# A state-space layer and its MLP on one Trainium2 core: B and C in buffers kept for the whole kernel, the identity written into them once, and a new table of priorities

## The chip, the cores and the metric

The kernel runs on one core of a Trainium2 chip. The figure of merit is device time in microseconds for one execution, the median of several. Engines are named as the profile names them: PE is TensorE's matmuls, PEld its weight loads, DVE is VectorE, ACT is ScalarE, POOL is GpSimd, SP is SyncE, whose queue (SPq) issues every transfer here.

## The reference

A chunked state-space recurrence for 4 batches x 8 heads x 768 positions, head width 32, state width 16, followed by an MLP on the 3072 x 256 result. Cut to what matters:

```python
cum = np.cumsum(log(a) in the chunk)
L = np.exp(cum[:, None] - cum[None, :]) * causal
M = (C @ B.T) * L                       # within a chunk
y = M @ x + (C @ state) * exp(cum)      # plus what the state brings in
state = exp(sum) * state + sum_j B_j x_j * exp(cum_last - cum_j)
h = y_all @ w_in                        # 256 -> 2048
out = (h - np.tanh(h)) @ w_out          # 2048 -> 256
```

## The kernel before

**Tiling.** A batch's 768 positions are cut into 7 chunks of 112 (the last has 96), 28 chunks in all. A chunk uses all 128 partitions: 112 are its positions, and the first 16 rows are the 16 state dimensions. So one matmul with 128 rows of weights gives both the part within the chunk and what the state brings in. To make that work, the tile of B, which is 128 columns wide, starts with a 16 x 16 identity, and columns 16 to 127 hold B transposed.

**Groups.** Two chunks form a group (CPG = 2, 14 groups). For each group four kinds of input are loaded: `bc` (B and C transposed, four transfers of 16 partitions each, line 301), `x` (313), `braw` (B with positions on partitions, 322). Three buffers each go round (NGB = 3). In `prep`, POOL writes the identity into the group's freshly landed `bc` (line 410) and multiplies `braw` by the decay into `bw` (403).

**One chunk.** PE forms the differences of the summed logarithms and C times B into `att` (lines 516 and 525; 454 and 466 for the first three chunks), ACT takes the exponential (540; 473), DVE multiplies (544; 478), POOL applies the causal mask (547; 483), and PE forms the outputs and the next state in `y` (573, 579). ACT copies the state into rows 0 to 15 of the next chunk's `x` (584) and rounds the outputs into `xh` (597); DVE forms the remainder `xl` (602). This is a recurrence: a chunk's `y` needs the copies of the one before.

**The MLP.** Weights arrive as 64-bit numbers, 512 KB a transfer in two transfers for each of 8 steps (`raw`, line 332), and ACT and DVE take them apart into high and low parts (`conv`: ACT 355 and 376, DVE 360, 365, 368, 372, 379). For a tile of 256 positions and a step, PE forms `ph` with 12 matmuls (650), ACT and DVE form g, its high part and its remainder (665, 669, 673, 680), and PE adds 12 matmuls into `o` (725). The first tile's first two steps work in plain float32 (634, 706) from `whole` (590). The first four tiles sweep over the steps in pairs while the later weights are still being converted; the other eight tiles run all steps at once.

**Order.** Every operation is first recorded with a cost in `Order`; `schedule` runs a list schedule over the recorded costs and lags with a priority for each operation, taken from its position plus the number in the table `RANK`; instructions are then written out in the order of the planned starts. Where the plan leaves a lull on PE in its first 65 us, `fill` writes small matmuls of ones without use (441) into the program. All waits between engines are put in by what each instruction reads and writes.

**The start.** ACT needs the clipped decays `a_sb` (DVE line 829) for the logarithm `la` (865); PE sums them (892, 897) behind a run of warming matmuls (859); DVE cuts the sums into three parts (904 to 908) which go out to memory and come back as `lt_c` and `rt_c` (911, 917, 919). POOL sets `lt_c` to ones first (852) and copies the identity `idn` into the three `braw` (847).

Of the kernel before, what the change touches and what calls it, by code (L numbers as in the profile page):

```python
# [9 lines left out]
F32 = mybir.dt.float32  # L10
# [9 lines left out]
P = 128  # L20
# [11 lines left out]
CPG = 2  # L32
# [19 lines left out]
57 373 306 52 13 1164 287 241 205 13 1206 343 161 1190 1241 114 367 108 1133 277 1199 243 1269 127 4 207 264 311 328  # L52
321 1175 105 167 330 1110 262 116 217 1141 -38 182 221 104 385 262 549 591 1114 142 276 81 79 1077 98 -9 99 1225 1080
508 155 398 226 39 277 1079 972 54 25 713 -51 1136 437 15 103 540 476 45 212 1093 244 173 438 53 580 176 -12 1038 -73
149 88 1035 -60 69 -5 -54 855 -93 560 1115 107 -10 956 -50 122 -89 142 247 41 -29 959 93 1159 800 26 -102 1047 -97 -3
1136 1104 1025 1118 217 1141 1062 -118 90 51 -67 456 1051 125 1050 923 1126 -69 240 437 133 1088 703 755 978 -16 1135
1112 -113 355 1087 1137 969 46 228 -115 967 1086 213 -4 6 172 158 991 151 983 181 1002 5 999 14 995 -120 37 -15 376
329 -91 -20 991 1026 1018 1081 1052 5 987 -80 339 -87 1021 1011 -184 -123 -164 123 -9 933 -1 -118 1078 -128 991 -82
-154 286 176 -45 -109 -147 843 915 -128 -102 -182 -161 944 119 713 1014 -115 1016 968 -179 5 90 811 -203 -2 141 -163
-135 1030 1013 64 -146 93 100 265 298 -195 1051 7 -169 -7 -168 114 977 -26 -63 -227 87 -57 -138 -119 1022 13 -69 -212  # L60
55 -244 473 -125 868 -158 -252 -209 253 451 523 961 -191 919 982 -20 -228 554 -148 -5 -196 -72 -274 -271 56 -257 76
-45 941 355 -251 839 848 841 -253 61 770 16 -241 -188 -5 726 -29 95 -237 668 -153 -269 989 893 836 908 -96 981 -248
-167 972 -208 -177 936 -85 -308 908 -317 48 916 -64 -60 -72 -136 -130 15 940 -50 -110 916 -221 -33 -309 61 952 -179
-77 857 280 869 24 -49 921 -277 242 -256 -18 -239 -255 941 -135 923 801 -332 816 -41 563 788 -181 -191 -304 -363 -89
-16 -268 817 -245 873 870 898 913 -26 835 -251 -300 -261 -134 884 898 433 240 867 -368 755 93 -163 883 439 -58 -111
179 763 -173 -194 -348 -391 791 -101 824 56 -376 -343 -285 -299 806 842 218 -353 577 -242 790 -298 -39 -350 226 -118
-40 -174 -34 -179 27 131 479 -160 840 -187 -283 114 806 -220 -234 384 96 -341 729 -407 779 -279 44 -20 -276 189 -369
-305 583 -280 -191 -403 768 795 768 -421 833 -70 736 -418 825 -75 -245 -296 386 -346 696 -352 792 666 -4 745 -220 683
-284 772 -463 -307 -104 232 -123 -49 -245 -226 650 -132 -387 -304 -284 704 -279 -289 -82 -298 -163 -176 249 700 -119
-325 -426 -240 -391 -227 -192 52 -294 -330 -205 -164 651 713 -148 34 226 -286 -3 -432 267 -250 676 -377 757 -366 612  # L70
-240 -251 713 -277 648 648 733 628 -442 510 -484 739 278 744 694 -502 -298 643 688 -116 569 74 -224 -269 -478 511 718
698 -469 101 112 -336 252 475 -324 400 572 613 485 694 -377 -244 553 50 -208 -339 -341 287 -335 -291 236 246 -151 -167
57 137 570 206 -109 -148 -259 324 509 -242 -454 194 -248 -253 -299 -445 -245 -431 -313 615 -116 -102 -471 -316 576
-334 -373 549 512 -367 -285 -262 488 -195 -449 308 -142 156 -301 506 -171 -258 359 -18 264 283 -501 -159 -147 -338
-355 33 189 -198 -163 -267 -240 -315 -198 230 215 150 216 -335 -277 -269 -248 -237 -264 -193 -286 -238 -260 -258 549
12 -479 150 508 518 -216 535 147 39 -279 -274 283 288 282 290 -296 -278 -272 -271 -270 -281 -286 -270 -270 -265 -265
-280 -277 -267 -264 -264 -264 -281 -279 -264 -264 -261 -258 -483 -448 -607 -365 -367 -409 442 -556 -494 196 22 -423
530 436 497 -420 -511 434 -401 471 -294 -291 -279 -278 -276 -273 -291 -288 -275 -274 -270 -269 -286 -283 -273 -271
-270 -267 -284 -281 -269 -268 -259 -258 -591 -212 -460 -599 -547 -436 -560 -437 68 405 -289 -278 -277 268 273 267 274
-289 -278 -276 -274 -270 -286 -291 -276 -273 -271 -270 -315 -157 -350 -55 -396 -134 -309 -89 -46 -332 -243 412 -227  # L80
375 359 -279 475 399 -109 154 490 499 -684 121 -310 -304 -296 -295 -293 -292 -305 -303 -293 -291 -290 -288 -305 -304
-288 -288 -286 -283 -297 -270 -269 -271 -270 -287 -284 -296 -291 -281 -309 -305 -291 -290 -279 -278 -306 -303 -280
-277 -272 -268 -298 -294 -280 -276 -271 -269 -292 -255 -253 -252 -252 -258 -256 -271 -268 -264 -160 -142 -142 -139
-152 -142 -150 -138 -118 -112 355 391 -133 -111 -312 -299 -298 214 221 213 224 -313 -301 -301 -299 -297 -307 -313 -297
-295 -286 -283 -309 -306 -287 -286 -285 -283 -305 -301 -285 -285 -284 -281 -299 -263 -261 -261 -259 -283 -281 -283
-279 -272 -304 -302 -295 -294 -291 -289 -303 -302 -287 -284 -277 -272 -301 -296 -274 -272 -268 -267 -295 -290 -275
-272 -268 -267 -290 -247 -247 -245 -247 -252 -250 -268 -262 -259 -168 -159 -168 -159 -167 -160 -167 -160 -114 -107
-638 -410 -151 -107 -306 -296 -298 131 141 133 143 -308 -298 -298 -296 -295 -305 -310 -291 -290 -281 -278 -306 -301
-280 -279 -279 -278 -300 -297 -280 -280 -279 -277 -293 -272 -268 -265 -261 -256 -295 -293 -285 -283 -277 -271 -294
-292 -269 -269 -264 -263 -288 -280 -265 -265 -262 -261 -280 -274 -265 -260 -246 -245 -277 -256 -254 -254 -253 -258  # L90
-256 -274 -270 -266 -153 -142 -151 -143 -150 -141 -150 -144 -99 -91 -624 -202 -140 -90 -295 -283 -282 54 63 54 65 -295
-277 -277 -275 -273 -290 -296 -274 -272 -268 -265 -289 -252 -252 -252 -252 -257 -253 -275 -269 -263 -295 -292 -274
-269 -260 -259 -289 -284 -261 -257 -255 -252 -281 -276 -254 -252 -246 -242 -273 -235 -235 -235 -234 -257 -255 -252
-248 -245 -279 -273 -253 -250 -243 -242 -269 -261 -243 -242 -236 -235 -261 -258 -245 -243 -236 -230 -256 -212 -212
-211 -208 -217 -215 -230 -228 -223 -262 -251 -251 -25 -15 -21 -13 -265 -253 -249 -246 -242 -255 -266 -243 -240 -231
-229 -255 -251 -231 -229 -227 -225 -252 -248 -227 -226 -225 -223 -243 -203 -203 -202 -204 -223 -223 -222 -219 -213
-250 -244 -237 -236 -230 -227 -244 -243 -227 -225 -218 -215 -242 -236 -217 -214 -209 -208 -236 -232 -218 -216 -210
# [9 lines left out]
class Order:  # L107
# [70 lines left out]
    def lag(self, a, b):  # L178
        if a == "DMA":
            return {"POOL": 2.4, "DVE": 1.3, "ACT": 1.3}.get(b, self.DMA_LATENCY)  # L180
# [851 lines left out]
```

## Time and profile before

| | us |
|---|---|
| median of 3 runs (332.73 to 334.93) | 333.41 |
| the profiled execution's own time | 334.76 |
| span of its profile | 333.1 |
| PE busy in the span | 325.3 (98%) |
| DVE, ACT, POOL busy | 226.6, 191.1, 57.8 |

The span runs from the first to the last instruction; the execution's own time has 1.66 us beside it. Ends of matmuls are modelled, so a busy PE also holds useless matmuls and short pauses. The granted clock of PE is 1.00 (2.4 GHz) in every slice.

### The profile page before, as it was taken

To read this page: it belongs to the slowest core of one execution; us is meant where nothing else is said; L and a number is where in the kernel's file an instruction comes from. 1 tells how busy PE (TensorE), PEld (TensorE's weight loads), DVE (VectorE), ACT (ScalarE), POOL (GpSimd) and SP (SyncE) were. 2 spreads that over 40 slices of the span, in tenths; PEclk is the share of its full clock that TensorE was granted. 3 is DMA by queue.
4 is the path that set the end of the run, shared out by engine and by line. 5 is a ranking of instruction groups with operands and counts; after the bars stand their busy time and mean duration, and the time that the engine had idled before them with its cause. 6 is when DMAs were issued, how large, how long until landed. Compare 5 with 4: busy or idle time off the path is not lost.

```text
span 333.1 us, 9055 instructions
## 1 busy us (share of the span) xinstructions
PE 325.3 (98%) x3864; PEld 312.4 (94%) x3864; DVE 226.6 (68%) x330; ACT 191.1 (57%) x404; POOL 57.8 (17%) x74
## 2 busy tenths in 40 slices
PE   8988999999999999999999999999999999999995
PEld 6976789899999999999999999999999999999995
DVE  5699999998899966555555755655655655654542
ACT  4876888885655655444535744644655645643441
POOL 8355446320002110100001201101111101100000
PEclk9999999999999999999999999999999999999999
DMA  6959579731001202200001200200100100000000
GB/s 176 237 158 281 126 197 268 202 124 40 3 9 37 64 0 75 70 31 2 31 2 32 65 22 10 65 9 24 63 2 3 34 2 2 31 2 2 31 2 32
DMA packets 12472, 21.41 MB, mean 64 GB/s; under 512 B 2848, under 2 KB 7648, under 8 KB 12432
## 3 DMA queue, kind: packets, MB, share of 16 engines
q1 hardware_dynamic: 12432, 20.84, 22.1%
q8 instruction: 30, 0.49, 0.7%
q14 instruction: 10, 0.08, 0.1%
HBM read 17.51 MB, written 3.32 MB: 63 GB/s over the span
## 4 chain that ended last, share of the span: by engine, by line
PE 82%; DMA 7%; DVE 3%; SPq 3%; ACT 2%; issue 1%; ACTq 0%; DVEq 0%
PE ph L650 36%; PE o L725 34%; DMA raw<-w_d 4%; DMA bc<-bc_d 3%; PE y L573 3%; PE att L525 2%; PE o L718 2%; PE att L718 2%; PE cp L454 1%; PE att L516 1%; SPq L332 1%; SPq L301 1%; SPq L917 1%; PE y L579 1%; DMA a_sb<-a_d 1%
## 5 line engine op out<-in xcount | busy, mean ns | idle before, releaser
L669 DVE TENSOR_TENSOR g<-ph,g 128x512 f32<-128x512 f32 x96 | 65.9, 690 | 54.0 <-ACT g L665 53.8
L665 ACT ACTIVATE g<-ph 128x512 f32<-128x512 f32 x96 | 57.5, 599 | 74.0 <-PE ph L650 72.7
L650 PE MATMUL ph<-xh,wh 128*128 128x256 f32 x376 | 95.5, 279 | 0.4 <-DVE g L669 0.3
L650 PE MATMUL ph<-xh,wl 128*128 128x256 f32 x376 | 94.6, 276 | 0.0
L680 DVE TENSOR_TENSOR gl<-g,gh 128x512 fp32r<-128x512 f32 x94 | 65.5, 699 | 26.3 <-ACT gh L673 24.5
L673 ACT CAST gh<-g 128x512 fp32r<-128x512 f32 x94 | 58.1, 620 | 33.6 <-DVE g L669 30.8
L650 PE MATMUL ph<-xl,wh 128*128 128x256 f32 x376 | 73.2, 276 | 0.0
L650 PEld LDWEIGHTS ph<-xh,wh 128*128 128x128 f32 x376 | 70.6, 188 | 1.1 <-DVE g L669 0.7
L650 PEld LDWEIGHTS ph<-xh,wl 128*128 128x128 f32 x376 | 70.6, 188 | 0.0
L547 POOL TENSOR_SCALAR_AFFINE_SELECT lt<-lt 128x896 f32<-128x896 f32 (+1 forms) x25 | 27.2, 1087 | 173.0 <-DVE lt L544 160.2
L650 PEld LDWEIGHTS ph<-xl,wh 128*128 128x128 f32 x376 | 56.6, 188 | 0.0
L725 PE MATMUL o<-gh,wh 128*128 128x256 f32 x344 | 55.0, 282 | 0.0
L725 PE MATMUL o<-gh,wl 128*128 128x256 f32 x344 | 53.0, 276 | 0.0
L725 PE MATMUL o<-gl,wh 128*128 128x256 f32 x344 | 53.0, 276 | 0.0
L725 PEld LDWEIGHTS o<-gh,wh 128*128 128x128 f32 x344 | 45.5, 188 | 0.9
L725 PEld LDWEIGHTS o<-gh,wl 128*128 128x128 f32 x344 | 45.4, 188 | 0.0
L725 PEld LDWEIGHTS o<-gl,wh 128*128 128x128 f32 x344 | 45.4, 188 | 0.0
L544 DVE TENSOR_TENSOR lt<-att,lt 128x896 f32<-128x896 f32 (+1 forms) x25 | 26.6, 1065 | 2.6 <-ACT lt L540 2.1
L540 ACT ACTIVATE lt<-att 128x896 f32<-128x896 f32 (+1 forms) x25 | 22.6, 903 | 2.3 <-PE att L525 1.5
L584 ACT COPY x<-y 16x64 f32<-16x64 f32 x96 | 19.5, 203 | 6.2 <-DVE xl L602 3.2
L403 POOL TENSOR_TENSOR bw<-braw,wdec 128x256 f32<-128x256 f32 x14 | 12.7, 913 | 48.4 <-PE y L579 43.1
L573 PE MATMUL y<-lt,x 128*32 128x112 f32 (+1 forms) x448 | 16.3, 263 | 1.1 <-POOL lt L547 0.7
(93 smaller groups left out, 305.1 us busy)
## 6 DMA issues: line engine op xcount, KB each, us to landing
raw<-w_d SPq DMA_DIRECT2D x16, 512.0 KB
x<-x_d SPq DMA_DIRECT2D x14, 256.0 KB
bc<-bc_d SPq DMA_DIRECT2D x56, 60.0 KB
out_d<-ob SPq DMA_DIRECT2D x16, 128.0 KB
braw<-bn_d SPq DMA_DIRECT2D x14, 112.0 KB
out_d<-pt SPq DMA_DIRECT2D x8, 128.0 KB
cum<-parts SPq DMA_DIRECT2D x1, 168.0 KB
lt_c<-cum SPq DMA_DIRECT2D x4, 27.0 KB
```

The lines of the kernel that those rows point to most:

```text
L540: nc.scalar.activation(k["l"][:, :, 0:q].rearrange("p (i w) q -> p i w q", i=4), place[1][:, :, 0:2, N : N + q], AF.Exp)
L544: nc.vector.tensor_tensor(out=lt, in0=place[1][:, :, 2:4, N : N + q], in1=lt, op=ALU.mult)
L547: nc.gpsimd.affine_select(out=k["l"][:, :, 0:q], in_=k["l"][:, :, 0:q], pattern=[[0, H], [1, q]], compare_op=ALU.is_ge, fill=0.0, base=N, ...
L573: nc.tensor.matmul(out=y[D * h : D * h + D, hg * Q : hg * Q + q], lhsT=d["x"][:, cg, P * hg + D * h : P * hg + D * h + D], rhs=k["l"][:, 4 ...
L584: nc.scalar.copy(grp[(ck + 1) // CPG]["x"][0:N, (ck + 1) % CPG, 2 * D * i : 2 * D * i + 2 * D], k["y"][D * i : D * i + N, H * D : H * D + ...
L650: nc.tensor.matmul(out=ph[:, j, :], lhsT=w_[:, u, 0, k, j * P : (j + 1) * P], rhs=d[("xh", "xl")[p]][:, k, ts], start=p == 0 and k == 0 an ...
L665: nc.scalar.activation(g, gs[t, u][0], AF.Tanh)
L669: nc.vector.tensor_tensor(out=g, in0=ph, in1=g, op=ALU.subtract)
L673: nc.scalar.copy(gh, gs[t, u][1])
L680: on.tensor_tensor(out=gl, in0=g, in1=gh.bitcast(F32), op=ALU.subtract)
L718: nc.tensor.matmul(out=halves[e], lhsT=(wh, wl, wh)[k][:, u, 1, j, e * P : (e + 1) * P], rhs=(gh, gh, gl)[k][:, j, :], start=u == seg[0] a ...
L725: nc.tensor.matmul(out=po[t, seg][:, e, :], lhsT=w_[:, u, 1, j, e * P : (e + 1) * P], rhs=g[:, j, :], start=u == seg[0] and k == 0 and j = ...
```

## The change

The three `bc` buffers become tiles of the constant pool that stay for the whole kernel, laid out as two halves x two chunks x (128 + 112) columns: B's 128 columns with the identity in the first 16, and C's 112 behind. POOL writes the identity once into all three, near the start (`beside`). The fourteen copies in `prep` go. A transfer now brings 4 runs of 224 numbers (896 bytes) for each partition instead of one of 960 (3840 bytes). The recorded lag from a transfer to an operation other than POOL, DVE and ACT becomes 1.2 instead of 0.8, and the table `RANK` has other numbers and fewer of them.

```diff
 RANK = """
-57 373 306 52 13 1164 287 241 205 13 1206 343 161 1190 1241 114 367 108 1133 277 1199 243 1269 127 4 207 264 311 328
...
+124 176 146 114 265 79 304 288 100 21 511 230 42 126 213 329 -6 99 792 241 121 151 359 114 161 243 136 137 209 171
...
         if a == "DMA":
-            return {"POOL": 2.4, "DVE": 1.3, "ACT": 1.3}.get(b, self.DMA_LATENCY)
+            return {"POOL": 2.4, "DVE": 1.3, "ACT": 1.3}.get(b, 1.2)
...
-        d["n_bc"] = slot("bc", NGB)
+        d["n_bc"], d["bc"] = slot("bc", NGB), bcs[G % NGB]
 
         def fn(i):
-            if i == 0:
-                d["bc"] = p2.tile([P, 2, CPG * (P + Q)], F32, tag="bc", name=f"bc{G}", bufs=NGB)
-            nc.sync.dma_start(out=d["bc"][32 * i : 32 * i + N], in_=bc[G, i])
+            nc.sync.dma_start(out=d["bc"][32 * i : 32 * i + N, :, :, N:], in_=bc[G, i])
...
-        def fn_c():
-
-            bb = d["bc"][:, :, 0 : CPG * P].rearrange("p w (c m) -> p w c m", c=CPG)
-            nc.gpsimd.tensor_copy(out=bb[:, :, :, 0:N], in_=idn.unsqueeze(1).unsqueeze(1).broadcast_to([P, 2, CPG, N]))
-
-        op("POOL", 0.38, fn_c, r=["idn"], w=[d["n_bc"]])
...
-        bb = d["bc"][:, :, c * P : (c + 1) * P]
-        cc = d["bc"][:, :, CPG * P + c * Q : CPG * P + (c + 1) * Q]
-        return bb, cc
+        return d["bc"][:, :, c, 0:P], d["bc"][:, :, c, P:]
...
-        return [grp[ck // CPG]["n_bc"], l_c[s], r_c[s]]
+        return [grp[ck // CPG]["n_bc"], "ci", l_c[s], r_c[s]]
...
+    bcs = [cp.tile([P, 2, CPG, P + Q], F32, name=f"bc{i}") for i in range(NGB)]
...
+    def beside():
+
+        for t in bcs:
+            nc.gpsimd.tensor_copy(out=t[:, :, :, 0:N], in_=idn.unsqueeze(1).unsqueeze(1).broadcast_to([P, 2, CPG, N]))
+
+    op("POOL", 1.5, beside, r=["idn"], w=["ci"])
```

**Where instructions move.** The orders of the two programs differ little over most of their length; the chunks 11 to 15 come later on PE, behind more of the MLP's matmul groups. The three places below are in the first part of the program. Numbers behind a name tell one tile from another.

First place, SP at the program's start. Before:

```order
L817 DMA a_sb<-a_d 112x192
L301 DMA bc_130<-bc_d 16x960
L819 DMA a_sb<-a_d 96x32
L313 DMA x_133<-x_d 128x512
L313 DMA x_143<-x_d 128x512
L301 DMA bc_130<-bc_d 16x960 x3
L322 DMA braw_99<-bn_d 112x256
L332 DMA raw_150<-w_d 128x1024 x2
L301 DMA bc_159<-bc_d 16x960 x4
```

Now:

```order
L294 DMA bc_102<-bc_d 16x4x224
L802 DMA a_sb<-a_d 112x192
L804 DMA a_sb<-a_d 96x32
L315 DMA braw_99<-bn_d 112x256
L325 DMA raw_132<-w_d 128x1024 x2
L294 DMA bc_102<-bc_d 16x4x224 x3
L306 DMA x_144<-x_d 128x512
L306 DMA x_146<-x_d 128x512
L294 DMA bc_103<-bc_d 16x4x224 x4
```

The two transfers of the first weights (`raw`) stand ahead of three of the four pieces of the first `bc` and of the first two `x`; before, they stood behind them all.

At the same place POOL, before:

```order
L821 IOTA pid 128x2
L822 IOTA ncol 128x16
L824 MEMSET upto 128x128
L825 AFFINE_SELECT upto<-upto 128x128
L824 MEMSET after 128x128
L825 AFFINE_SELECT after<-after 128x128
L852 MEMSET lt_c 128x896
L852 MEMSET lt_c 128x2304
L847 COPY braw_99<-idn 16x256
L847 COPY braw_100<-idn 16x256
L847 COPY braw_101<-idn 16x256
L410 COPY bc_130<-idn 128x2x2x16
```

Now:

```order
L837 MEMSET lt_c 128x896
L837 MEMSET lt_c 128x2304
L806 ISA
L806 IOTA pid 128x2
L807 IOTA ncol 128x16
L809 MEMSET upto 128x128
L810 AFFINE_SELECT upto<-upto 128x128
L809 MEMSET after 128x128
L810 AFFINE_SELECT after<-after 128x128
L832 COPY braw_99<-idn 16x256
L832 COPY braw_100<-idn 16x256
L832 COPY braw_101<-idn 16x256
```

The two settings of `lt_c` to ones stand at the front, ahead of the constants `pid`, `upto` and `after`; the identity's copies into the three `bc` follow the last row shown.

Second place, DVE from the identity on to the first chunks. Before:

```order
L838 TENSOR_SCALAR idn<-ncf,pidf 128x16
L829 TENSOR_SCALAR a_sb<-a_sb 128x224
L875 TENSOR_SCALAR rt_c<-lt_c,par 128x3200 x2
L906 CAST parts<-rows 112x2x128
L908 TENSOR_TENSOR rest<-rows,parts 112x256
L906 CAST parts<-rest 112x2x128
L904 TENSOR_TENSOR parts<-rest,parts 112x2x128
L360 TENSOR_SCALAR wm_216<-raw_150 128x512
L478 TENSOR_TENSOR lt_189<-att,lt_189 128x448 x2
L365 TENSOR_SCALAR wv_220<-wv_220 128x512
L368 SCALAR_TENSOR_TENSOR wm_216<-wv_220,wm_216 128x512
L478 TENSOR_TENSOR lt_233<-att,lt_233 128x448
```

Now, first the clipping of `a_sb`, which stands ahead of the small constants:

```order
L800 MEMSET a_sb 32x32
L814 TENSOR_SCALAR a_sb<-a_sb 128x224
L817 TENSOR_SCALAR pid<-pid 128x1
L818 TENSOR_SCALAR pid<-pid 128x1
L819 CAST pidf<-pid 128x2
L820 CAST ncf<-ncol 128x16
```

and then from the parts of the sums on:

```order
L897 CAST parts<-rows 112x2x128
L899 TENSOR_TENSOR rest<-rows,parts 112x256
L897 CAST parts<-rest 112x2x128
L895 TENSOR_TENSOR parts<-rest,parts 112x2x128
L358 TENSOR_SCALAR wv_185<-wv_185 128x512
L353 TENSOR_SCALAR wm_202<-raw_132 128x512
L361 SCALAR_TENSOR_TENSOR wm_202<-wv_185,wm_202 128x512
L365 SCALAR_TENSOR_TENSOR wv_185<-wv_185,wm_202 128x512
L353 TENSOR_SCALAR wm_202<-raw_132 128x512
L463 TENSOR_TENSOR lt_192<-att,lt_192 128x448 x2
L463 TENSOR_TENSOR lt_239<-att,lt_239 128x448
```

Five instructions of the first conversion (`wv`, `wm`) stand between the parts and the first multiplication of a chunk (`lt`), where one stood before.

Third place, PE from the second chunk's outputs to the first matmul with `rt_c`. Before:

```order
L573 MATMUL y_331<-lt_233,x_133 32x112 x8
L579 MATMUL y_331<-x_133,bw_222 16x32 x8
L441 MATMUL pq_195<-const-float32-1.0 32x128 x12
L573 MATMUL y_382<-lt_286,x_143 32x112 x8
L579 MATMUL y_382<-x_143,bw_319 16x32 x8
L441 MATMUL pq_195<-const-float32-1.0 32x128 x5
L516 LDWEIGHTS lt_c
L516 MATMUL att<-rt_c,lt_c 128x2x112
```

Now:

```order
L557 MATMUL y_334<-lt_239,x_144 32x112 x8
L563 MATMUL y_334<-x_144,bw_213 16x32 x8
L426 MATMUL pq_183<-const-float32-1.0 32x128 x17
L557 MATMUL y_400<-lt_280,x_146 32x112 x8
L563 MATMUL y_400<-x_146,bw_369 16x32 x8
L501 LDWEIGHTS lt_c
L501 MATMUL att<-rt_c,lt_c 128x2x112
```

The useless matmuls (`const-float32-1.0`) between the second and the third chunk's outputs are 17 instead of 12, and the five behind the third chunk are gone. In the whole program they are 30 instead of 28, beside the ten that warm.

## Rows read from the trace of the kernel before

**Rows 1.** Busy time by stage: one row is a stretch of the span (us from its start), its length, then for each engine its busy us and (x) the instructions it started, then the granted TensorE clock, the mean busy share of the 16 DMA engines and GB/s.

```profile
0.00:10.00 10.00, 8.58 (x39) 7.46 (x40) 6.34 (x17) 4.67 (x9) 6.85 (x16) 1.00 0.67 204
10.00:20.00 10.00, 9.06 (x158) 7.77 (x157) 7.58 (x14) 8.28 (x33) 5.31 (x8) 1.00 0.78 194
20.00:30.00 10.00, 9.62 (x133) 8.01 (x135) 9.46 (x12) 7.64 (x21) 4.94 (x6) 1.00 0.75 226
30.00:40.00 10.00, 8.85 (x165) 7.02 (x157) 9.83 (x13) 8.22 (x18) 4.41 (x5) 1.00 0.64 159
...
40.00:62.00 22.00, 21.81 (x384) 19.90 (x383) 21.41 (x28) 17.58 (x40) 13.35 (x12) 1.00 0.86 228
...
140.00:300.00 160.00, 160.00 (x1866) 156.68 (x1865) 91.22 (x136) 84.31 (x175) 13.66 (x17) 1.00 0.08 23
```

**Rows 2.** TensorE's instructions in order of time up to the first large matmul of the MLP, selected: start us, us, engine, line, operation, output <- inputs, forms, how many were merged into the row, and in brackets idle time before it and what ended it.

```profile
0.84 4.44 PE L859 MATMUL warm<-const-float32-1.0 128*32 128x128 f32 x20 [0.84 <-PEq L1022]
5.86 1.16 PE L892 MATMUL pr<-upto,la 128*112 128x128 f32 x4 [0.58 <-ACT la L865]
...
17.49 0.71 PE L466 MATMUL att<-bc 16*128 16x112 f32 x16 [0.55 <-POOL bc L410]
...
19.16 0.59 PE L573 MATMUL y<-lt,x 128*32 128x112 f32 x16 [0.39 <-ACT whole L590]
...
19.68 2.83 PE L441 MATMUL pq<-const-float32-1.0 128*32 128x128 f32 x24
22.38 0.59 PE L573 MATMUL y<-lt,x 128*32 128x112 f32 x16
...
22.99 1.16 PE L441 MATMUL pq<-const-float32-1.0 128*32 128x128 f32 x9
24.09 0.27 PE L516 MATMUL att<-rt_c,lt_c 9*128 9x224 bf16 x4
...
27.12 1.99 PE L634 MATMUL ph<-whole,wv 128*128 128x256 f32 x8 [0.38 <-DVE wv L372]
...
30.86 1.99 PE L706 MATMUL o<-g,wv 128*128 128x256 f32 x8 [0.45 <-DVE g L669]
...
39.13 0.59 PE L573 MATMUL y<-lt,x 128*32 128x112 f32 x16 [0.70 <-POOL lt L547]
...
39.77 0.38 PE L650 MATMUL ph<-xh,wh 128*128 128x256 f32 x1
```

**Rows 3.** VectorE's instructions in order of time, selected; the columns are those of rows 2.

```profile
3.63 1.44 DVE L829 TENSOR_SCALAR a_sb<-a_sb 128x224 f32<-128x224 f32 x1 [1.43 <-DMA a_sb<-a_d]
...
8.21 0.29 DVE L906 CAST parts<-rows 112x256 bf16<-112x256 f32 x1 [0.95 <-ACT rows L902]
...
9.90 0.43 DVE L360 TENSOR_SCALAR wm<-raw 128x512 uint32<-128x512 uint32 x1
11.68 0.62 DVE L478 TENSOR_TENSOR lt<-att,lt 128x448 f32<-128x448 f32 x1 [1.36 <-ACT lt L473]
13.33 0.63 DVE L478 TENSOR_TENSOR lt<-att,lt 128x448 f32<-128x448 f32 x1 [1.02 <-PE att L466]
...
14.33 0.94 DVE L368 SCALAR_TENSOR_TENSOR wm<-wv,wm 128x512 uint32<-128x512 uint32 x1
...
25.84 1.23 DVE L372 SCALAR_TENSOR_TENSOR wv<-wv,wm 128x1024 uint32<-128x1024 uint32 x1
```

**Rows 4.** GpSimd's instructions in order of time, selected.

```profile
2.09 2.84 POOL L852 MEMSET lt_c<- 128x896 bf16 x2
4.89 2.62 POOL L847 COPY braw<-idn 16x256 f32<-16x256 f32 x3
...
16.53 0.42 POOL L410 COPY bc<-idn 128x64 f32<-128x64 f32 x1
```

**Rows 5.** SyncE's queue in order of time, selected: each row is the issue of one or more transfers (x2: two).

```profile
2.18 0.90 SPq L313 DMA_DIRECT2D x<-x_d  x2
3.12 1.35 SPq L301 DMA_DIRECT2D bc<-bc_d  x3
...
4.98 0.90 SPq L332 DMA_DIRECT2D raw<-w_d  x2
...
12.30 0.35 SPq L332 DMA_DIRECT2D raw<-w_d  x1
...
15.11 0.42 SPq L332 DMA_DIRECT2D raw<-w_d  x1
```

**Rows 6.** The DMA queue's own line (packets, MB, share of 16 engines over the stretch) for two stretches in which one kind of transfer makes up nearly all bytes. From 97 to 104 us: the four pieces of one group of B and C, 64 packets of 3840 bytes, with as many of 4 bytes. From 329 to 333 us: the last two stores of the output, 256 packets of 1024 bytes and 32 small ones.

```profile
q1 hardware_dynamic: 128, 0.25, 13.9%
...
q1 hardware_dynamic: 288, 0.26, 19.3%
```

**Rows 7.** One turn of the recurrence in the packed part, from the launch of one chunk's outputs (line 573) to that of the next: TensorE, VectorE and GpSimd.

```profile
234.65 0.59 PE L573 MATMUL y<-lt,x 128*32 128x112 f32 x16
...
235.81 1.09 DVE L544 TENSOR_TENSOR lt<-att,lt 128x896 f32<-128x896 f32 x1 [0.33 <-ACT lt L540]
...
236.97 0.98 POOL L547 TENSOR_SCALAR_AFFINE_SELECT lt<-lt 128x896 f32<-128x896 f32 x1 [0.83 <-DVE lt L544]
...
238.04 0.39 DVE L602 TENSOR_TENSOR xl<-y,xh 128x224 fp32r<-128x224 f32 x1 [0.24 <-ACT x L584]
...
241.60 0.59 PE L573 MATMUL y<-lt,x 128*32 128x112 f32 x16
```

## What was predicted

> **What bounds the kernel now.** I read the busy times by stage first, then PE's own idle times, then whoever ends them. From 140 to 300 us PE is busy 160.00 of 160 us [rows 1], and in the stretch from 40 to 62 us it is busy 21.81 of 22. So from about 40 us on the kernel is a fixed list of matmuls, and the change neither adds nor removes one of the MLP. What can move the end is when that list begins: the first large matmul of the MLP starts at 39.77 us [rows 2]. Everything before it is a start-up in which PE waits, in three ways: idle (the bracketed times of rows 2), useless matmuls written into the program (24 instructions from 19.68 us, 9 from 22.99 us), and warming. What it waits for is DVE above all, busy 9.46 and 9.83 of 10 us from 20 to 40 us; between 10 and 20 us only 7.58 [rows 1]. The DMA engines are 64 to 78% busy there, near enough to full to matter.
>
> **The sum is made against the profiled execution**: span 333.1 us, own time 334.76 us. The median of the three timed runs is 333.41 us, 1.35 us under that execution. I take the gain from the span and subtract it from the median. A change of less than 1%, 3.33 us, is about what a measurement of this kernel can't tell from no change.
>
> **Part 1: the copies of the identity.** Fourteen POOL copies go, three come. POOL is at most half busy in the start [rows 1], so their own time is worth nothing; what counts is where one stood between a transfer and PE. That is once: the copy at 16.53 us takes 0.42 us, and PE's `att` at 17.49 us stood idle 0.55 us for it [rows 4, 2]. That wait can go wholly, for the matmul now waits for the transfer alone: 0.55 us. The three new copies lie behind the `braw` copies, near 8 us, while PE wants the first `bc` near 11 us: nothing, covered by PE's work on the sums. Without that cover they would cost three times 0.42 us.
>
> **Part 2: transfers in short runs.** A transfer of B and C brings 57 KB in 64 runs of 896 bytes instead of 61 KB in 16 of 3840. The first half of rows 6 gives 0.139 x 16 x 7 us over 64 packets, 243 ns for one of 3840 bytes; the second gives 0.193 x 16 x 4 us over 256, 48 ns for one of 1024 bytes (a store, the nearest row) [rows 6]. Four short ones are 193 ns: no dearer. That end is a gain of 50 ns an engine and transfer. At the other end each of the three more runs costs a whole 48 ns beside the bytes, 144 ns a transfer; eleven such transfers stand ahead of the second weights' last half, so these would land 1.6 us later. I take zero, since the row with 1024 bytes is the nearer, and the other end can cost what part 6 gains.
> A page of the Trainium skill speaks against this part: "DMA: Bandwidth & Descriptors", section "Why small descriptors are slow (HBM only)", has about 3 cycles of overhead for each packet beside its 32-byte beats. By that, an estimate from its figures, 28 beats would cost 31 and 120 would cost 123, so the same bytes would take some 8% longer, the second weights would land 0.2 us later, and the sum would be 1.8 instead of 2.0 us. Rows 6 show no such loss.
>
> **Part 3: the first microseconds.** DVE's clipping of `a_sb` takes 1.44 us at 3.63 us, though a longer one-input operation (128x512, 9.90 us) takes 0.43 [rows 3]. POOL's two settings of `lt_c` run from 2.09 to 4.93 us [rows 4], and the clipping ends 0.14 us behind them: it was held. Now they stand first on POOL, and should run from about 0.9 to 3.7 us. The clipping then ends near 4.0 instead of 5.07 us, and the logarithm follows. PE gains less than that: it stood idle only 0.58 us before `pr`, since it warms until 5.28 us [rows 2]. So 0.58 us, and DVE gets the sums that much earlier, too.
> For the three new copies a rule of the Trainium skill would give another price: "SBUF — State Buffer", section "SBUF: two separate sides", says that GpSimd and a VectorE operation in a two-port mode hold one pair of ports in turn, each for its whole instruction. The clipping's 1.44 us agrees with it. By the rule each new copy could hold up DVE once for its 0.42 us, 1.26 us in all; 0.95 of them fall where DVE waits for the sums anyway, so the sum would be 0.3 us less. No row shows three copies in a row beside DVE's work, and I leave it out.
>
> **Part 4: DVE's order.** Before, DVE stood idle 1.36 and 1.02 us for the first chunk's two multiplications, and 0.95 us for the sums [rows 3]. Now the first half of the first conversion stands in that place: five instructions, by rows 3 about 0.43 + 0.43 + 0.94 + 0.7 + 0.43 = 2.9 us of work (the 0.7 is a little over half of the 1.23 us that 1024 columns take). They can fill it if the weights are there: `raw` is now issued about 2.3 us earlier than at 4.98 us, since two `x` and three pieces of `bc` (2.25 us of issuing) follow it instead of standing ahead [rows 5]. So DVE is ahead by 2.4 us, and 0.6 more from part 3. PE can't take that at once. Its wait of 0.39 us at 19.16 us, for `whole`, goes as ACT now copies that first. Up to the second chunk's outputs PE so gains 0.58 + 0.55 + 0.39 = 1.52 us.
>
> **Part 5: useless matmuls.** By rows 2 the 24 instructions from 19.68 us end with the third chunk's outputs at 22.38 us: 0.11 us each, and two for each matmul. One matmul more stands ahead of the second chunk's outputs, 0.22 us; so these start at 19.16 - 1.52 + 0.22 = 17.86 us. Behind them stand 17 instead of 12, which begin 0.52 us later as before, at 18.38, and take 34 x 0.1125 = 3.83 us: the third chunk's outputs start at 22.2, where 22.38 stood. But the five behind it are gone, so the first matmul with `rt_c` comes 0.61 us behind, at 22.8 instead of 24.09 us. The path is 1.3 us shorter here, if the mask of the third chunk is ready by then.
>
> **Part 6: up to the packed part.** Three idle times of PE are left, all for DVE directly or through POOL: 0.38, 0.45 and 0.70 us [rows 2], 1.53 in sum. DVE is ahead by about 3 us, PE by 1.3. So DVE's lead exceeds PE's, and these should shrink; but DVE also depends on PE (its multiplications wait for `att`), and the second weights, issued at 12.30 and 15.11 us [rows 5], are limited by DMA bandwidth, as the bytes ahead of them are the same. I take half of it, 0.7 us; the ends are 0 and 1.53.
>
> **Part 7: the rest.** Chunks 11 to 15 come later on PE. From `y` to `xl`'s end takes 3.8 us, and to the next mask's end 3.3 us, in a turn of 6.95 us [rows 7]; the new turns are no shorter than this one, so nothing is lost. In exchange DVE is freed in the stretch up to 100 us, which gains nothing since PE is packed.
>
> Sum: 1.3 + 0.7 = 2.0 us. Span 331.1, median **331.4 us**.
>
> **The rivals.**
> *The start gains nothing.* The 17 useless matmuls are in the program, whatever the engines do. If the second chunk's outputs come at 19.16 us as before, the third's come at 23.5, and only the loss of the five afterwards brings it back. For it: the DMA engines move about 200 GB/s in the first 20 us [rows 1] and the bytes up to the second weights are the same. Against: the idle times of rows 2 have causes that the order takes away. 333.3 us.
> *All idle goes.* The 1.3 us, the whole 1.53 instead of half of it, and 0.5 to 1 us of pauses that the modelled ends hide in PE's busy time: 3.3 to 3.8 us, 329.8 us. For it: DVE's lead of 3 us is larger than what is asked of it. Against: DVE and ACT would have to be ahead at every one of these places.
> *The first `bc` comes late: slower.* Three of its four pieces now queue behind two weight transfers of 512 KB; at the first slice's 204 GB/s [rows 1] these take 5.1 us, so the pieces land near 10.5 us and the two `x` 2.5 us later. PE wants `bc` near 11 us. It decides from a landing at 12.5 us on: then `att`, the first multiplications, the outputs and every later chunk move back together, and the filler after them still runs. Two or three us late, less part of the other gains, with a few more idle times: 335.2 us.
>
> **How the numbers follow.** My forecast has a chance of 0.54, nothing gained 0.22, all idle gone 0.14, late `bc` 0.10. The forecast's own spread (parts 2 and 6, 0 to 1.53) is 330.6 to 332.6. The range reaches to the neighbours: 329.7 to 334.5, which leaves out the larger part of the last case. Faster by over 1% (under 330.1) is most of the third case and a little of the first, 0.15; slower by over 1% (over 336.7) only the tail of the last, 0.05; within, 0.80.
>
> **What would show it.** Right: the clipping of `a_sb` at 0.3 to 0.5 us; no idle time of PE ahead of `pr`; no idle time of DVE over 0.5 us between the parts and the first multiplications; the third chunk's outputs near 22 us; the first large matmul at 37.5 to 38 us; from there on the same packed list. Wrong: a first `att` that waits for a transfer, DVE waiting for weights, the first large matmul at 39 us or later, or gaps on PE in the packed part, above all where chunks 11 to 15 now stand.

## The result, and the profile after

The changed kernel takes **337.94 us** (median of 22 runs) where the kernel before took 334.07 beside it; the ratio is 1.009, 95% interval 1.007 to 1.0111 (it leaves out executions over 1.5% above a kernel's fastest, seven of the 22, and so lies below the quotient of the medians). The forecast was 331.4, and the range ended at 334.5. The profiled execution has a span of 336.1 us and 337.81 us of its own, against 333.1 and 334.76: 3.0 us more.

The busy times by stage, with the columns of [rows 1]:

```profile
10.00:20.00 10.00, 9.29 (x164) 8.39 (x164) 9.24 (x16) 8.16 (x31) 6.42 (x9) 1.00 0.76 206
...
40.00:62.00 22.00, 19.25 (x301) 17.29 (x298) 18.60 (x24) 14.26 (x32) 6.55 (x8) 0.92 0.59 173
```

DVE is busy 9.24 us from 10 to 20 us instead of 7.58, as forecast. But the stretch from 40 to 62 us, in which PE stood still for 0.19 us before, now has 2.75 us without work and a mean granted clock of 0.92. TensorE's rows from 5 to 65 us, selected:

```profile
5.29 0.85 PE L883 MATMUL pr<-upto,la 128*112 128x128 f32 x4
...
17.57 0.59 PE L557 MATMUL y<-lt,x 128*32 128x112 f32 x16 [0.60 <-ACT x L568]
...
18.18 3.83 PE L426 MATMUL pq<-const-float32-1.0 128*32 128x128 f32 x33
21.98 0.59 PE L557 MATMUL y<-lt,x 128*32 128x112 f32 x16
...
22.62 0.27 PE L501 MATMUL att<-rt_c,lt_c 9*128 9x224 bf16 x4
...
28.84 1.99 PE L690 MATMUL o<-g,wv 128*128 128x256 f32 x8 [0.55 <-DVE g L653]
...
37.64 0.59 PE L557 MATMUL y<-lt,x 128*32 128x112 f32 x16 [0.51 <-DVE xl L586]
...
38.27 0.38 PE L634 MATMUL ph<-xh,wh 128*128 128x256 f32 x1
...
51.89 0.62 PE L709 MATMUL o<-gl,wh 128*128 128x256 f32 x4
54.33 0.25 PE L501 MATMUL att<-rt_c,lt_c 9*128 9x224 bf16 x1 [1.82 <-DMA braw<-bn_d]
54.98 0.25 PE L501 MATMUL att<-rt_c,lt_c 9*128 9x224 bf16 x1 [0.40 <-DMA rt_c<-cum]
55.51 0.25 PE L501 MATMUL att<-rt_c,lt_c 9*128 9x224 bf16 x1 [0.28 <-DMA rt_c<-cum]
55.94 0.25 PE L501 MATMUL att<-rt_c,lt_c 9*128 9x224 bf16 x1 [0.18 <-DMA rt_c<-cum]
...
58.50 1.05 PE L709 MATMUL o<-gh,wl 128*128 128x256 f32 x4
```

Up to 38.27 us this is the forecast's story: the first large matmul comes 1.5 us sooner than in [rows 2] (how much of that is the order's: see the account of the prediction below). Then the matmul of chunk 10 stands still for 2.68 us in four pieces. It is the first to use the second part of `rt_c` (chunks 10 to 27), which comes in four transfers; each piece of the wait ends with one of them. (The first is put down to a `braw`, which this matmul doesn't read; it too is a `rt_c`.) And behind the wait four matmuls take 1.05 us instead of 0.62. The granted clock of PE in that place (columns: stretch, length, PE busy and instructions, clock, DMA share, GB/s):

```profile
54.00:56.00 2.00, 0.81 (x7) 1.00 0.36 84
56.00:57.00 1.00, 1.00 (x33) 0.94 0.34 92
57.00:58.00 1.00, 1.00 (x26) 0.50 0.69 148
58.00:59.00 1.00, 1.00 (x7) 0.50 1.02 289
59.00:60.00 1.00, 1.00 (x7) 0.50 0.99 387
60.00:61.00 1.00, 1.00 (x9) 0.85 0.86 252
```

PE was idle most of the time from 52.4 to 55.9 us, and from 57 to 60 us it gets 0.50, which is 1.2 instead of 2.4 GHz. This is no single event: in 20 of the 22 executions the mean granted clock is 0.99 or 0.995, and the two with 1.00 took 333.97 and 335.87 us; of 68 executions of the kernel before, taken beside the experiments, 7 have 0.995 or less. Why the `rt_c` are late stands on SP's queue (start, us, line, transfers):

```profile
41.72 3.03 SPq L908 DMA_DIRECT2D lt_c<-cum  x4
44.86 2.05 SPq L294 DMA_DIRECT2D bc<-bc_d  x2
47.04 0.50 SPq L325 DMA_DIRECT2D raw<-w_d  x1
47.65 1.24 SPq L294 DMA_DIRECT2D bc<-bc_d  x2
48.98 0.54 SPq L306 DMA_DIRECT2D x<-x_d  x1
49.57 1.25 SPq L910 DMA_DIRECT2D rt_c<-cum  x4
```

SP issues without a break. Six transfers stand between `lt_c` and `rt_c`, four of them `bc`, and each `bc` takes longer to issue than it did (28 `bc` now stand ahead of the second `rt_c` in the whole program, 24 before). Before and after, all transfers of `bc` (minimum/median/maximum in ns):

```profile
L301 SPq DMA_DIRECT2D bc<-bc_d x56: 310/418/1629, 1.3 to 224.9; - x56
```

```profile
L294 SPq DMA_DIRECT2D bc<-bc_d x56: 560/567/1822, 0.8 to 228.2; - x56
```

So there are two suspects: 0.15 us more for each issue (the short runs), and the place that the new order gives the second `rt_c`.

### The profile page after: what moved, and what is told of

Its sections match the earlier page's. It is cut to its first block, busy times and chain, and to the rows that moved or that the text cites. A ratio compares the mean times of both kernels' runs of the same rounds, so it can differ in the third digit from the quotient of the medians.

```text
span 336.1 us, 9070 instructions
## 1 busy us (share of the span) xinstructions
PE 326.7 (97%) x3868; PEld 314.2 (94%) x3868; DVE 224.7 (67%) x330; ACT 191.7 (57%) x404; POOL 48.8 (15%) x63
## 4 chain that ended last, share of the span: by engine, by line
PE 86%; DMA 5%; DVE 4%; ACT 2%; SPq 1%; issue 1%; ACTq 0%; DVEq 0%
PE ph L634 37%; PE o L709 36%; PE y L557 4%; DMA raw<-w_d 3%; PE att L509 3%; PE o L702 2%; PE att L702 2%; DMA rt_c<-cum 2%; PE att L501 1%; PE pq L426 1%; ACT lt L458 1%; DVE lt L528 1%; PE y L563 1%; DVE lt L463 1%; DVE wl L372 1%
## 5 line engine op out<-in xcount | busy, mean ns | idle before, releaser
L664 DVE TENSOR_TENSOR gl<-g,gh 128x512 fp32r<-128x512 f32 x94 | 66.4, 708 | 24.2 <-ACT gh L657 22.0
L709 PE MATMUL o<-gh,wh 128*128 128x256 f32 x344 | 55.8, 284 | 0.0
L531 POOL TENSOR_SCALAR_AFFINE_SELECT lt<-lt 128x896 f32<-128x896 f32 (+1 forms) x25 | 25.9, 1035 | 163.4 <-DVE lt L528 150.5
L396 POOL TENSOR_TENSOR bw<-braw,wdec 128x256 f32<-128x256 f32 x14 | 9.7, 700 | 75.2 <-PE y L563 63.5
```

The costliest lines, as they stand in the source:

```text
L531: nc.gpsimd.affine_select(out=k["l"][:, :, 0:q], in_=k["l"][:, :, 0:q], pattern=[[0, H], [1, q]], compare_op=ALU.is_ge, fill=0.0, base=N, ...
L664: on.tensor_tensor(out=gl, in0=g, in1=gh.bitcast(F32), op=ALU.subtract)
L709: nc.tensor.matmul(out=po[t, seg][:, e, :], lhsT=w_[:, u, 1, j, e * P : (e + 1) * P], rhs=g[:, j, :], start=u == seg[0] and k == 0 and j = ...
```

## The experiments

Every time of before is the one taken beside the runs in question, 333.6 to 334.1 us.

**The suspects one by one.** First, long runs in the new order:

```diff
-nc.sync.dma_start(out=d["bc"][32 * i : 32 * i + N, :, :, N:], in_=bc[G, i])
+nc.sync.dma_start(out=d["bc"][32 * i : 32 * i + N], in_=bc[G, i])
...
```

The transferred rows hold the identity here, and the three copies that write it are left out.

> The changed kernel with B and C coming in 16 runs of 3840 bytes again: the identity's columns lie in the transferred rows (as constants), the three copies that write it are left out, and the order of all engines is that of the changed kernel. Theory A (issuing 64 runs costs SP 0.57 instead of 0.42 us, and that makes the second set of rt_c late): the issue is 0.42 us again; 11 transfers of B and C stand in SP's unbroken row from 34.9 us to the rt_c, so these are issued 11 x 0.15 = 1.7 us earlier and land at 52.5 to 54.2 instead of 54.2 to 55.9 us; PE's 2.7 us of idle shrink to about 1, the clock stays at 1.00, and the time is 333 to 334 us. Theory B (the new order puts the rt_c too late, whatever a transfer costs): issued less than 0.7 us earlier, 2 us of idle and the clock's fall stay, 337 us. Theory C (the DMA engines take longer over short runs, and the issue doesn't matter): the issue times stay where they are, but the rt_c land 1 us or more sooner after their issue than 4.6 us.

Measured: 335.35 us, ratio 1.001 (0.9977 to 1.0043). The issue's median is 370 ns, 0.2 us less than with short runs in the same order. SP and PE in the profiled execution:

```profile
43.63 1.25 SPq L910 DMA_DIRECT2D rt_c<-cum  x4
```

```profile
36.88 0.39 PE L634 MATMUL ph<-xh,wh 128*128 128x256 f32 x1
...
50.85 0.27 PE L501 MATMUL att<-rt_c,lt_c 9*128 9x224 bf16 x3
51.43 0.25 PE L501 MATMUL att<-rt_c,lt_c 9*128 9x224 bf16 x1 [0.31 <-DMA rt_c<-cum]
```

The `rt_c` were issued 5.9 us sooner, not 1.7: SP's delay builds up from the start (the second `lt_c` are 4.3 us sooner). That is about when the first of them was issued before (43.44 us), but PE now comes to chunk 10 some 2 us sooner. They took longer to land, and the last one still came 0.3 us late, so that the time missed theory A's 333 to 334 us. The first large matmul starts 1.4 us before that of the changed kernel. Short runs cost 2.6 us here (337.94 - 335.35). But 6 of 12 executions still had a mean clock of 0.985 to 0.995, at a median of 336.4 us against 333.5 for the others.

Second, the old priorities on the new operations:

```diff
-RANK = (the change's 1281 numbers)
+RANK = (the old numbers, without the 14 identity copies, one put in)
-return {"POOL": 2.4, "DVE": 1.3, "ACT": 1.3}.get(b, 1.2)
+return {"POOL": 2.4, "DVE": 1.3, "ACT": 1.3}.get(b, self.DMA_LATENCY)
```

> The change without its new order: kept buffers, identity written once, short runs, but the order's numbers are those of before (14 numbers of the identity copies left out, one put in) and the delay from a transfer to PE is 0.8 us again in the planner. Theory A: SP loses 0.15 us with each transfer of B and C, but before the rt_c landed 2.4 us ahead of PE's need, so most of it is hidden: 333.5 to 335 us, less 0.5 us for the identity copy. Theory B: as before, 333 to 334 us. Theory C: transfers land later everywhere in the start: 336 us or more.

Measured: 342.25 us, ratio 1.0255 (1.0227 to 1.0283). Only theory C's open end (336 us or more) holds that. Taking the short runs away, with the rows of the first experiment, changed nothing:

> The kernel with the change's buffers but the old order's numbers, which took 342.25 us, with runs of 3840 bytes (identity in the transferred rows, no copies of it): the old order with nothing of the short runs. If short runs (issue and landing) cost those 8 us: 333 to 334 us, some tenths under the kernel before for the identity copy that PE waited for. If the kept buffers cost them (a transfer that waits for something that a fresh buffer didn't): 340 us or more.

Measured: 342.07 us, 1.0246 (1.0212 to 1.0279). So these 8 us belong to neither the runs nor, as the exact order below shows, the buffers. The priorities choose among what is ready in a list schedule; with fourteen operations gone they give another sequence on every engine, and PE idles here and there up to 65 us. The test was no test of the layout.

Third, the place of the second `rt_c` on SP alone, in the changed kernel:

```diff
 _, start = self.plan()
+first, then = self.second
+for k, i in enumerate(then):
+    start[i] = max(start[j] for j in first) + 0.01 * (k + 1)
...
```

The two names stand for the second `lt_c` and the second `rt_c`.

> The changed kernel with one thing moved: on SP the four second transfers of rt_c stand directly behind those of lt_c instead of behind five more pieces of B and C, weights and x. Theories A and B alike: issued from about 44.8 to 46 us, landing by 51.2 us, before PE's need at 52.4; the 2.7 us of idle go, the granted clock stays at 1.00 there, which gives back some 2 us more, and the time is 332 to 333.5 us, if the pieces that now come 1.3 us later aren't missed. If the late rt_c isn't what lost the time, 337 us, with PE idle elsewhere.

Measured: 334.74 us, ratio 1.0004 (0.9979 to 1.0029). PE and POOL:

```profile
53.10 0.28 PE L507 MATMUL att<-rt_c,lt_c 9*128 9x224 bf16 x4
...
61.67 0.59 PE L563 MATMUL y<-lt,x 128*32 128x112 f32 x16 [0.89 <-POOL lt L537]
```

```profile
56.56 0.65 POOL L400 TENSOR_TENSOR bw<-braw,wdec 128x256 f32<-128x256 f32 x1 [3.81 <-DMA braw<-bn_d]
```

The wait for `rt_c` is gone and the clock stays at 1.00; 3.2 us come back. The forecast of 332 to 333.5 us is missed all the same, for now the next late transfer shows: a `braw`, for which POOL's queue waits, and the mask behind it costs PE 0.89 us. SP is still behind.

Fourth, the fall of the clock alone. The changed kernel, with useless matmuls where PE waits:

```diff
+    def warm_wait(ck):
+        one = nc.const_aps.tensor(1.0, (P, P), F32)
+        for _ in range(16 * (ck == SPAN[1].start)):
+            nc.tensor.matmul(out=place[1][0:32, 0, 0, 0:P], lhsT=one[:, 0:32], rhs=one, start=True, stop=True)
...
-        op("PE", 0.84, lambda: (differences(ck), ...
+        op("PE", 0.84, lambda: (warm_wait(ck), differences(ck), ...
```

> The changed kernel with sixteen useless matmuls (32 rows of ones, 128 columns) ahead of the first matmul that needs the second rt_c, some 3.6 us of work in the 3.5 us from 52.4 to 55.9 us that PE waits there. They compute nothing that is read. They separate the wait from the clock. If the fall of the granted clock to 0.50 from 57 to 60 us follows from PE's idle time: the clock stays at 1.00, the four-matmul groups there take 0.62 instead of 1.05 us, and the time falls by 1.5 to 2.5 us to 335.5 to 336.5 though nothing lands earlier. If the clock falls for another reason, or the wait is all: 338 us or more.

Measured: 336.69 us, ratio 1.0082 (1.0054 to 1.011).

```profile
52.74 3.74 PE L515 MATMUL att<-const-float32-1.0 128*32 128x128 f32 x32
56.41 0.27 PE L501 MATMUL att<-rt_c,lt_c 9*128 9x224 bf16 x4
...
58.28 0.62 PE L714 MATMUL o<-gh,wl 128*128 128x256 f32 x4
```

PE starts chunk 10 0.5 us later than without them, and yet its span is 1.3 us shorter (334.8): the groups take 0.62 us, and the clock is 1.00. Five of its six executions have a mean clock of 0.999 or 1.00, where 2 of 22 had without the useless matmuls. So the fall of the clock followed from PE's idle time. Its price is less sure: by the rows of the granted clock above, the half speed costs 0.06 + 3 x 0.5 + 0.15 = 1.7 us; the medians differ by 1.25, but the ratios only by 0.001, and their intervals overlap. By these rows the wait of 2.7 us is the larger part.

**Both repairs together** (long runs, `rt_c` first):

> Both repairs together: the changed kernel with runs of 3840 bytes (identity in the transferred rows) and with the second rt_c directly behind the second lt_c on SP. With long runs alone these rt_c were issued at 43.6 us and the last landed at 51.4, 0.3 us too late; now they are issued some 3 us earlier. If both causes add (the issue of short runs, the place in the order): no wait of PE there and none for braw at 61 us, since with short issues nothing behind is late; the clock stays at 1.00 in nearly all executions, and the time is 331.5 to 333 us, faster than before by 0.5% or a little more. If long runs alone already gave all there is: 334 us, scattered like that kernel's 331.6 to 337.

Measured: **332.51 us**, ratio 0.9963 (0.9939 to 0.9986), the best of all. No wait stands at chunk 10 (its matmul runs from 51.45 us) nor at 61 us, and 11 of 12 executions had a clock of 0.999 or 1.

**What short runs cost without the new order.** First in the kernel before, with padded buffers:

```diff
-p2.tile([P, 2, CPG * (P + Q)], F32, tag="bc", ...)
+p2.tile([P, 2, CPG, P + Q + 4], F32, tag="bc", ...)
...
```

> The kernel before with one thing changed: the rows of its buffers for B and C are padded by 4 columns in each chunk, so that a transfer has 64 runs of 960 bytes instead of 16 of 3840; bytes, order and identity copies are as before. Theory A: the issue on SP goes from 0.42 to 0.57 us; the second rt_c come about 1 us later, which their 2.4 us of slack cover; first stages move by a few tenths: 334 to 335 us. Theory B: no change, 334 us. Theory C: the DMA engines' busy time of this queue rises by over 10%, and transfers in the start land later: 335 us or more.

Measured: 346.6 us, 1.0368 (1.0332 to 1.0404). Twelve microseconds, nearly all lost evenly from 62 us to the end, where no `bc` matters. So the padding was suspected, and not the runs. Two kernels part them, short runs without padding and a shift without short runs:

```diff
-nc.sync.dma_start(out=d["bc"][32 * i : 32 * i + N], in_=bc[G, i])
+nc.sync.dma_start(out=d["bc"][32 * i : 32 * i + N, :, :, 1:], in_=bc[G, i, :, :, :, 1:])
...
```

```diff
+gap = p3.tile([P, 48], F32, tag="gap", name="gap", bufs=1)
```

> The short runs in the kernel before again, with no buffer made larger: the buffers keep their 3840 bytes a partition in the order of the changed kernel (each chunk's B beside its C), and each run leaves out the first of 240 columns, which the identity copy writes anyway, so that a transfer has 64 runs of 956 bytes. Order and copies are as before. In the padded kernel the matmuls of 256 columns followed each other by 0.119 instead of 0.113 us from 62 us to the end, which gave some 11 of its 12.5 us. Theory P (that came from where the padding put the other tiles in SBUF): the step is 0.113 us again here, and what is left is the price of short runs with the old order: 334.5 to 337 us. Theory Q (the loss belongs to the short runs): 0.119 us and 346 us again.

> The kernel before with one unused tile of 192 bytes a partition, which moves xh, xl, g, gh and gl in SBUF by 192 bytes, as the padded kernel did; weights, transfers and order are as before. If the place of the matmuls' moving operands sets their step (theory P): 0.119 instead of 0.113 us from 40 us on, and 344 to 346 us. If it was something else of the padded kernel: 334 us.

Measured: 335.68 us, 1.0055 (1.0034 to 1.0077), without padding, and 344.84 us, 1.0352 (1.0327 to 1.0378), with 192 unused bytes and nothing else. In the second, from 140 to 300 us:

```profile
140.00:300.00 160.00, 160.00 (x1785) 1.00 0.08 23
```

In the same sequence of instructions there were 1866 before [rows 1]: PE gets through 4.3% fewer at full granted clock. The gap moves the tiles of one pool, the moving operands `xh`, `xl`, `gh` and `gl` among them; which of these does it was not separated. It has nothing to do with the change, where matmuls of 256 columns still follow each other by 0.113 us from 140 to 300 us. Without the padding, short runs cost the kernel before 1.7 us.

**The change without its order**, with every engine's sequence written out exactly as before, for short and for long runs:

```diff
-span, start = self.schedule([i + d for i, d in enumerate(ahead)])
+start = [int(w) / 1e5 for w in START.split()]
...
```

`START` holds the starts in the plan of before.

> The change without its order, now really so: kept buffers, identity written once, short runs, and each engine's instructions in exactly the sequence of before (the start times of the plan of before are written out; with the old priorities alone the planner made another sequence, which took 342 us with short and with long runs alike). Theory A: the short runs alone cost what they cost in the kernel before (335.7 us, 0.55% up), less up to 0.5 us for the identity copy that PE waited for: 335 to 336 us. Theory B (short runs harmless, the new order did it all): 333.5 to 334 us.

> The same exact old sequence with kept buffers and with runs of 3840 bytes (the identity's columns come in the rows, no copies of it). All that is left of the change is that fourteen identity copies are gone. Both theories: 333.4 to 334 us, at best 0.5 us under the kernel before; a larger gain would mean that the copies held up more than the one wait of 0.55 us.

Measured: 334.50 us, 1.0036 (1.0013 to 1.0059), with short runs; 333.04 us, 0.9984 (0.9959 to 1.0008), with long ones. The first lies between the two theories, the second at the best that was expected, 0.5 us under the kernel before. SP's first microseconds, short and then long:

```profile
3.54 1.86 SPq L342 DMA_DIRECT2D bc<-bc_d  x3
...
7.01 3.11 SPq L342 DMA_DIRECT2D bc<-bc_d  x5
10.17 0.58 SPq L363 DMA_DIRECT2D braw<-bn_d  x1
```

```profile
3.12 1.35 SPq L342 DMA_DIRECT2D bc<-bc_d  x3
...
5.92 2.28 SPq L342 DMA_DIRECT2D bc<-bc_d  x5
8.25 0.42 SPq L363 DMA_DIRECT2D braw<-bn_d  x1
```

After nine `bc` SP is 1.9 us behind, 0.2 us for each: a transfer behind a short-run `bc` takes longer to issue as well (the `braw`, 0.58 instead of 0.42 us). The queue's own share in the two:

```profile
q1 hardware_dynamic: 15120, 20.61, 22.0%
```

```profile
q1 hardware_dynamic: 12432, 20.84, 22.6%
```

That is 73.4 us of 333.8 with short runs and 75.0 of 331.7 with long ones. The DMA engines are no busier over short runs; what is lost is lost in the issue. The delay reaches PE through a `raw`, for which DVE waits 0.81 us at 32 us and ACT then 1.97 us; ACT's copies of the state stand behind that conversion in its order:

```profile
36.84 1.14 ACT L396 ACTIVATE wv<-raw 128x1024 f32<-128x1024 f32 x1 [1.97 <-DMA raw<-w_d]
```

With long runs the same conversion starts at 36.00 us without a wait. PE's last wait before the MLP, short and then long:

```profile
39.52 0.86 PE L605 MATMUL y<-lt,x 128*32 128x112 f32 x16 [1.76 <-DVE xl L634]
```

```profile
39.00 0.59 PE L605 MATMUL y<-lt,x 128*32 128x112 f32 x16 [0.70 <-POOL lt L579]
```

Behind the longer wait the granted clock falls in this kernel too:

```profile
40.00:43.00 3.00, 3.00 (x36) 0.50 0.53 132
```

So PE is 0.5 us behind at this place and 2.1 us behind at chunk 10 (55.43 against 53.34 us). In the profiled execution with long runs the clock fell as well, elsewhere (0.83 from 10 to 20 us). Taking only executions with a mean clock of 0.999 or 1.00, the medians are 334.2 and 333.0 us: of the 1.5 us, 1.2 remain.

The medians in one table (us), with ratios:

| order of the instructions | 64 runs | 16 runs |
|---|---|---|
| exactly as before, kept buffers | 334.50 (1.0036) | 333.04 (0.9984) |
| the change's | **337.94** (1.0090) | 335.35 (1.0010) |
| the change's, second `rt_c` first on SP | 334.74 (1.0004) | 332.51 (0.9963) |

The ratios, in brackets, are to the kernel before that ran beside. Short runs cost 1.5 to 2.6 us by the medians of a row, 1.4 to 2.7 by its ratios; the place of `rt_c` costs 3.2 and 2.8 us by the medians of a column, 2.9 and 1.6 by its ratios. In the last row and in the last column the intervals of the two ratios overlap a little. The new order itself, with `rt_c` moved, differs from the old one by 0.2 and 0.5 us, which is within the noise.

## Why the prediction was wrong

**Part 2, short runs: this step failed.** It priced the packets on the DMA engines, between 0 and 1.6 us, took zero, and for the engines zero was right. It never asked what a transfer of 64 runs costs SP, though [rows 5] show what one of 16 does (three in 1.35 us), and though 56 of them pass one queue. The price is 0.15 to 0.2 us each, and 1.5 to 2.6 us at the end. Before the change no row had such an issue; a bound from below zero to a few tenths for each of some 28 transfers ahead of the second `rt_c` would have held it.

**Part 7, the rest: failed too.** "PE is packed" was read from the kernel before, where the second `rt_c` were in time: its matmul runs without a wait at 53.50 us. The part looked at the recurrence and not at what PE needs from memory in that stretch. The new order issues the `rt_c` as one block behind four more `bc`, in a plan that counts 0.42 us for issuing each of these. From the first issue to the first use they took 4.8 us. Wait and clock together cost what the start had gained on the profiled execution of before and 3.0 us more. "Gaps on PE in the packed part" stood among the signs of a wrong prediction, but it was put where chunks 11 to 15 stand, and it came at chunk 10.

**Part 3 was right.** POOL's settings of `lt_c` end at 3.60 us; the clipping behind them starts at 4.13 and takes 0.38 instead of 1.44 us, and PE no longer waits ahead of `pr`. (It ends at 4.51 and not near 4.0, since `a_sb` landed later; with long runs it starts at 3.65.) The rule weighed there (the Trainium skill, "SBUF — State Buffer", section "SBUF: two separate sides": GpSimd and a two-port VectorE operation hold a pair of ports in turn) agrees with that 0.38. The price of 1.26 us for the three new copies does not show: of DVE's operations beside them one is clearly longer than in the kernel with long runs, which has no such copies, by 0.2 us (`wm`, 1.21 instead of 1.01).

**Parts 4 and 5 came out by number, and in good part by luck.** DVE has no gap where it had three, the second chunk's outputs come at 17.57 us (forecast 17.86), the third's at 21.98 (22.2), the first `rt_c` matmul at 22.62 (22.8). But PE waits 0.60 us for ACT ahead of the second chunk's outputs, which the forecast didn't have. And the gain was counted against a slow start of one execution. The kernel with the unused tile has the instructions and the order of before; the profile before, then this one:

```profile
7.56 2.95 PE L454 MATMUL cp<-upto,la 128*128 128x112 f32 x16
```

```profile
6.71 1.94 PE L455 MATMUL cp<-upto,la 128*128 128x112 f32 x16
...
17.92 0.59 PE L574 MATMUL y<-lt,x 128*32 128x112 f32 x16 [0.39 <-ACT whole L591]
...
22.84 0.27 PE L517 MATMUL att<-rt_c,lt_c 9*128 9x224 bf16 x4
...
38.50 0.39 PE L651 MATMUL ph<-xh,wh 128*128 128x256 f32 x1
```

Without the change, that is, the second chunk's outputs came at 17.92 us, the first `rt_c` matmul at 22.84 and the first large matmul at 38.50, where [rows 2] have 19.16, 24.09 and 39.77 and the changed kernel has 17.57, 22.62 and 38.27. In the profiled execution of before PE's first matmuls simply took longer; why, the rows don't show (the granted clock stands as 1.00 there). The prediction noted that this execution was 1.35 us above the median, read its gain of 1.3 us off it, and still subtracted that from the median: a second fault of the sum. Two other profiles in the old order (short runs without padding; kept buffers with long runs) were quick there, had a fall of the clock between 12 and 16 us, and started the first large matmul at 39.63 and 39.64, so a start sooner or later by 1.2 us is within the spread of one order.

**Part 1**: the wait for the identity copy went. (POOL was not at most half busy in the start, as the part says: [rows 1] have 6.85 of the first 10 us. It cost nothing that shows.) With the exact old order and long runs, where little else is left of the change, the median is 0.5 us under before, as forecast, but the interval (0.9959 to 1.0008) holds zero.

**Part 6 was mis-sized because of part 2.** It allowed 0.7 us; from 24 to 38 us the lead on [rows 2] grows only from 1.47 to 1.50. Three waits of 0.55, 0.31 and 0.51 us remain, all for DVE. With long runs the first large matmul starts at 36.88 us, and at 37.46 with `rt_c` first, better than the 37.5 to 38 forecast and 1.0 to 1.6 us ahead of the 38.50 in the old order. So the order gains something at the start, and short runs took nearly all of it; this rests on single profiles.

**The rivals.** The start gained little on the old order's 38.50 us, as the first rival had it, though not for its reason. The first `bc` was not late: `att` begins at 10.35 us. A slower kernel through a late transfer was the right kind of rival, at the wrong transfer; its price, 335.2 us, was too low, since it had no clock in it.

## What to carry over

A transfer has two prices, one on the engines that move it and one on the queue that issues it; when a layout cuts runs into pieces, multiply the second by all transfers on that queue and see which needed one stands last. "Packed" is a statement about one order: after a reordering, list every first use of a transferred tile in the packed part, and how long before it the issue stands. Before adding up the idle times of one profile, compare that execution with the median, and take a second profile if it is slow. And to test a layout without its order, write out the old sequence; old priorities on a changed list of operations are a third kernel.

## What was not expected of the hardware

Moving the pool with PE's moving operands by 192 bytes in SBUF costs 3.5% of the whole kernel: from one matmul of 256 columns to the next it is 0.119 instead of 0.113 us, with a granted clock of 1.00 throughout. A padding chosen for another reason can hide or fake any small effect.

The same slow step appears without such a cause: in the profiled execution of the best kernel, from 80 to 90 us, PE passes 87 instructions,

```profile
80.00:90.00 10.00, 10.00 (x87) 1.00 0.01 2
```

where the kernel with long runs alone, with nearly the same sequence, passes 91. It lasts from about 60 to 92 us there and costs, by 4 of 91 in 32 us, some 1.4 us. What brings it on wasn't found, and it may be part of the spread between executions.
